# A letter for each operation in place of one drawn number per visit, in the planner that orders an attention and gated feed-forward kernel

## The chip, the cores and the metric

The kernel runs on one core of a Trainium2 chip. The metric is the device time of one execution in microseconds (us). PE is the matrix engine (TensorE), DVE is VectorE, ACT is ScalarE, POOL is GpSimd, and SP is the engine that issues nearly all DMAs. PSUM has eight banks, and every product of PE lands in one of them.

## What is computed

The reference is attention with a threshold, followed by a gated feed-forward network on its output:

```
scores = scale * np.matmul(q, k.transpose(0, 1, 3, 2))
thresh = np.max(scores, axis=-1, keepdims=True) - tau
scores = np.where(scores >= thresh, scores, -1000000000.0)
attn = np.exp(scores - np.max(scores, axis=-1, keepdims=True))
attn = attn / (np.sum(attn, axis=-1, keepdims=True) + 1e-09)
x = np.matmul(attn, v), then transposed to (B * S, H * D)
gate = 1.0 / (1.0 + np.exp(-(x @ w_gate)))
out = gate * (x @ w_val) @ w_out
```

There are 8 batches of 8 heads, 576 positions and a head size of 64; the network has 4608 tokens, a width of 512 and 1536 hidden units. All is float32.

## The kernel before

The attention is cut into 32 visits, one for a pair of heads of one batch. A visit has nine tiles of 128 query rows. For each tile PE computes scores (L641) into two PSUM banks, DVE takes the maximum (L648), ACT the exponential (L662), and DVE applies the threshold mask and sums (L665). When the tiles of a group are done, PE transposes the masked rows (L756, again into two banks), ACT copies them out (L704), and at last PE multiplies by the values (L795). A pair of banks that holds scores is free for the next tile only when L665 has read it; a pair that holds transposes is free when L704 has read it.

The network runs in between: block 0 (one batch) in whole-array matmuls at L937, block 0's output and later outputs at L866, blocks 1 and 2 at L892 in half-array matmuls where two units run side by side, the first half of one beside the second half of the other. A unit is one accumulator bank. When an L892 unit ends, ACT (L995) or ACT and DVE (L998) read its bank, and a later unit starts in that bank; the tiny copy "seen" (L904, at L866 it is L875) marks such a turn. The last six batches use a seven-product scheme (L1213, L1355) in pairs; nearly all of it stands behind the last attention work.

The order is not written by hand. Every operation is recorded with an engine, an estimated cost, its inputs and outputs, and a key (`Plan.op`). `Plan.run` then plays the operations through on estimated costs: whenever an engine is free, the ready operation with the lowest key whose buffers and banks can be had is taken, and this fixes the instruction order of each of the five engines. The chip does not see keys or costs, only the five resulting queues, each of which runs in order, and the waits between them. Two constants belong to the planner alone: `LAG`, the time it adds when a result crosses to another engine, and `SWITCH`, what it charges when PE changes between row-halved, column-halved and whole-array matmuls. `vary` sets what is added to each key between 0 and 398: in the kernel before a uniform draw between -3 and 3 from a generator seeded once per visit (`ORDERS` holds the 32 seeds, and a seed of 0 adds nothing). A step of a key is about one tile. Operations of the network on PE have keys above a million and get nothing.

Of the kernel before, what the change touches and what calls it, by code (L numbers as in the profile page):

```python
# [4 lines left out]

# [39 lines left out]
class Plan:  # L45
# [53 lines left out]
        self.ops.append(o)  # L99
        return o  # L100

    def vary(self, seed):

        draw = random.Random(seed)
        self.nudge = (lambda: draw.uniform(-NUDGE, NUDGE)) if seed else lambda: 0.0

    def room(self, o):
        need = {}
# [47 lines left out]
    def run(self):  # L156
# [10 lines left out]
        while True:  # L167
# [52 lines left out]
            while events and events[0][0] <= now + 1e-9:  # L220
# [5 lines left out]
                else:  # L226
# [6 lines left out]
                    for s in x.succ:  # L233
                        lag = 0.0 if s.eng == x.eng else LAG[s.eng]
                        s.ready = max(s.ready, now + lag + s.lag)
# [55 lines left out]
def LO_DVE(j, out):  # L291
# [2 lines left out]

DVE_LO_IN, DVE_LO_OUT = (), ()

LAG = {"PE": 0.3, "DVE": 0.06, "ACT": 0.08, "POOL": 0.12, "SP": 0.08}

WARM = 16

# [3 lines left out]
    "s": [{0, 1}, {2, 3}, {4, 5}, {6, 7}],  # L304
    "b": [{6}, {7}, {4}, {5}, {2}, {3}, {0}, {1}],
}
STAY, SWITCH, TURN = 4, 0.15, 0.0615
S_CAP, T_CAP, L_CAP, MOE_CAP = (4, 3), 1, 1, 2

MM_HALVES = 0.234  # L310
WHOLE, FULL_STEP = (0,), 6

ORDERED, NUDGE = 398, 3.0
ORDERS = (
    9752, 0, 748, 1675, 6489, 1465, 5011, 3559, 9165, 5460, 4071, 9213, 3320, 7371, 6555, 4493,
    0, 1253, 2636, 4108, 9865, 7590, 738, 2276, 1215, 1549, 3530, 2072, 647, 565, 5179, 0,
)

def LATE(b, hp):
# [1285 lines left out]
```

## Time and profile before

| | us |
|---|---|
| median of 3 runs | 1307.7 |
| lowest and highest run | 1306.86, 1309.71 |
| profiled execution, its own time | 1305.66 |
| span of its instructions | 1303.6 |
| PE busy in the span | 1265.9 |
| DVE, ACT, POOL busy | 892.8, 685.4, 512.8 |

The span is what the profile's rows are counted in; it is 2.1 us shorter than the time of the same execution, and that execution is 2.0 us below the median. PE is busy for 97% of the span.

### The profile page before, as it was taken

The page shows a single profiled execution, that of the slowest core. Times are in us where ns is not written, and L with a number is a line of the kernel's source. Part 1 is how long each engine was busy: PE and PEld are TensorE (multiplying, and loading weights), DVE is VectorE, ACT ScalarE, POOL GpSimd, SP SyncE. Part 2 cuts the span into 40 slices and gives each one's busy share as a digit, 9 for nine tenths or more (in the row PEclk, how much of TensorE's full clock was granted, in tenths as well). Part 3 has the DMA queues.
Part 4 walks back from the last instruction along what each step waited for, and adds up shares of the span by engine and source line. Part 5 has one row for each costly group of instructions (what it writes and reads, how often), then busy time and mean ns, then how long its engine had stood idle before and what let it go on. Part 6 is the DMA issues. An engine that isn't in the chain of part 4 may idle for free.

```text
span 1303.6 us, 27638 instructions
## 1 busy us (share of the span) xinstructions
PE 1265.9 (97%) x10596; PEld 997.8 (77%) x10596; DVE 892.8 (68%) x1811; ACT 685.4 (53%) x1144; POOL 512.8 (39%) x501
## 2 busy tenths in 40 slices
PE   7879999999999999999999999999999999999998
PEld 5557777777777777777777767888888888888887
DVE  7878887576776766767777774548954579555494
ACT  6877776666665656665776651224522235312242
POOL 4567777665444366584868400111001100010100
PEclk8989999999999999999999999999999999999999
DMA  7669986677655767887446668666676666765663
GB/s 284 218 216 305 337 283 218 225 263 237 234 191 180 236 222 255 288 296 227 156 146 202 222 222 295 195 201 209 221 270 195 198 206 203 232 197 188 203 208 113
DMA packets 134571, 293.17 MB, mean 225 GB/s; under 512 B 27304, under 2 KB 62376, under 8 KB 134440
## 3 DMA queue, kind: packets, MB, share of 16 engines
q1 hardware_dynamic: 134296, 291.41, 67.5%
q8 instruction: 84, 1.38, 0.4%
q14 instruction: 47, 0.39, 0.1%
q10 hardware_dynamic: 144, 0.00, 0.0%
HBM read 229.34 MB, written 62.01 MB: 224 GB/s over the span
## 4 chain that ended last, share of the span: by engine, by line
PE 86%; DMA 3%; DVE 3%; POOL 2%; ACT 2%; issue 2%; SPq 1%; DVEq 0%; POOLq 0%; ACTq 0%
PE banks L1213 26%; PE banks L1355 13%; PE banks L795 11%; PE banks L892 11%; PE banks L641 10%; PE banks L756 5%; PE banks L866 5%; PE banks L937 4%; DMA rb<-rd 1%; DVE p L665 1%; ACT pt L704 1%; DMA xa<-xf 1%; DVE st L648 1%; DMA sod<-s_o 0%; DMA qp<-in_q_dram 0%
## 5 line engine op out<-in xcount | busy, mean ns | idle before, releaser
L648 DVE TENSOR_REDUCE st<-banks 128x1 f32<-128x576 f32 x256 | 190.3, 753 | 142.3 <-PE banks L641 136.5
L665 DVE SCALAR_TENSOR_TENSOR p<-banks,st,p 128x576 f32<-128x576 f32 x256 | 205.0, 813 | 25.2 <-ACT p L662 18.3
L641 PE MATMUL banks<-kp,qp 64*128 64x288 f32 x1280 | 204.2, 424 | 12.9 <-DVE p L665 6.5
L662 ACT ACTIVATE p<-banks,st 128x576 f32<-128x576 f32 x256 | 186.7, 742 | 49.8 <-DVE st L648 48.4
L1126 POOL TENSOR_TENSOR gA<-gA 128x512 f32<-128x512 f32 x18 | 24.2, 1347 | 412.9 <-DVE gA L1192 412.9
L892 PE MATMUL banks<-x,wi 64*128 64x512 f32 x1152 | 178.6, 423 | 3.5 <-DVE g L998 2.5
L1355 PE MATMUL banks<-gs_p,wo_p 128*128 128x512 f32 x756 | 172.3, 389 | 0.0
L1355 PEld LDWEIGHTS banks<-gs_p,wo_p 128*128 128x128 f32 x756 | 141.9, 188 | 29.4
L641 PEld LDWEIGHTS banks<-kp,qp 64*128 64x128 f32 x1280 | 113.5, 189 | 49.7 <-DVE p L665 14.5
L704 ACT COPY pt<-banks 128x1024 f32<-128x1024 f32 x128 | 129.5, 1012 | 35.3 <-PE banks L756 33.3
L892 PEld LDWEIGHTS banks<-x,wi 64*128 64x128 f32 x1152 | 111.3, 186 | 25.9 <-DVE g L998 5.1
L795 PE MATMUL banks<-pt,vs 128*64 128x256 f32 x1024 | 124.7, 386 | 5.6 <-DVE p L665 3.9
L756 PEld LDWEIGHTS banks<-ident,p 64*128 64x128 f32 x2304 | 98.2, 141 | 35.3 <-DVE p L665 5.1
L1150 DVE TENSOR_TENSOR qu<-banks,qp 128x512 f32<-128x512 f32 x72 | 49.8, 692 | 92.9 <-PE banks L1213 74.4
L756 PE MATMUL banks<-ident,p 64*128 64x64 f32 x2304 | 106.1, 227 | 6.1 <-DVE p L665 2.6
L1213 PE MATMUL banks<-xs_p,wa 128*128 128x512 f32 x432 | 110.2, 390 | 0.0
L1213 PE MATMUL banks<-xs_p,wt 128*128 128x512 f32 x432 | 109.2, 389 | 0.0
L795 PEld LDWEIGHTS banks<-pt,vs 128*64 128x64 f32 x1024 | 69.9, 138 | 47.2 <-DVE p L665 5.9
L1213 PE MATMUL banks<-xs_p,ws 128*128 128x512 f32 x432 | 104.1, 390 | 0.0
L1213 PEld LDWEIGHTS banks<-xs_p,wa 128*128 128x128 f32 x432 | 80.8, 188 | 17.8 <-issue 1.2
L1213 PEld LDWEIGHTS banks<-xs_p,ws 128*128 128x128 f32 x432 | 80.9, 188 | 17.5 <-issue 0.7
L1213 PEld LDWEIGHTS banks<-xs_p,wt 128*128 128x128 f32 x432 | 81.1, 188 | 16.9
(125 smaller groups left out, 1991.0 us busy)
## 6 DMA issues: line engine op xcount, KB each, us to landing
wi<-wid SPq DMA_DIRECT2D x48, 512.0 KB
qp<-in_q_dram SPq DMA_DIRECT2D x31, 640.0 KB
wa<-wid SPq DMA_DIRECT2D x36, 512.0 KB
ws<-sid SPq DMA_DIRECT2D x36, 512.0 KB
wt<-sid SPq DMA_DIRECT2D x36, 512.0 KB
wo_p<-sod SPq DMA_DIRECT2D x36, 512.0 KB
wo_p<-wod SPq DMA_DIRECT2D x27, 512.0 KB
vs<-in_v_dram SPq DMA_DIRECT2D x32, 384.0 KB
```

The source lines that it names most:

```text
L641: nc.tensor.matmul(s.ap[:, c, :HALF], vis.q1.ap[rows, x, c0 : c0 + P], vis.k1[x].ap[rows, kc : kc + HALF], start=x == heads[0][0], stop=x ...
L648: op("DVE", 0.76, key, lambda: nc.vector.tensor_reduce(out=st.ap[:, 0:1], in_=sv(), axis=AX.XY, op=ALU.max, negate=True), reads=[s], write ...
L662: op("ACT", 0.74, key, lambda: nc.scalar.activation(p(), sv(), AF.Exp, bias=st.ap[:, 0:1], scale=1.0), reads=[s, (st, 0)], writes=[(g.p, i)])
L665: mask = op("DVE", 0.9, key, lambda: nc.vector.scalar_tensor_tensor(out=p(), in0=sv(), scalar=st.ap[:, 1:2], in1=p(), op0=ALU.is_ge, op1=A ...
L704: op("ACT", act(n), key, lambda: nc.scalar.copy(dst(), src()), reads=at, writes=[part])
L756: nc.tensor.matmul(banks[z]()[:, m * D : (m + 1) * D], p.ap[rows, o : o + P], ident[rows, rows], is_transpose=True, start=m == 0, stop=m = ...
L795: nc.tensor.matmul(av.get()[h * D : (h + 1) * D, a:z], vis.vs.ap[:, j, h], m(h), start=i == 0, stop=i == len(ms) - 1, skip_group_check=True,)
L866: nc.tensor.matmul(acc.ap, w()[h], x()[h], start=start, stop=stop, skip_group_check=True)
L892: nc.tensor.matmul(acc.ap, w()[ROWS[z]], x()[ROWS[z]], start=e == 0 and z == 0, stop=e == n - 1 and z == 1, skip_group_check=True,)
L937: nc.tensor.matmul(m.ap, wv[:, a, c * P : (c + 1) * P], xs[c].ap[:, z, c0:c1], start=e == 0, stop=e == 11,)
L1213: nc.tensor.matmul(acc.ap, wv[:, y, (2 * h + c) * P : (2 * h + c + 1) * P], xt[prod][c].get()[:, z], start=e == 0 and prod in FIRST, stop= ...
L1355: nc.tensor.matmul(acc.ap, w.ap[:, e, c, y], gt[prod][2 * g + c].get()[:, z], start=m == 0 and g == 0 and prod in FIRST, stop=m == 5 and g ...
```

## The change

Each of the 32 entries of `ORDERS` becomes a string of letters. The n-th operation of a visit with a key between 0 and 398 gets the n-th letter, where m adds nothing, a takes 3 away and z adds 3.25, in steps of a quarter; past the end of the string nothing is added. The three visits whose seed was 0 now have letters too, and the last string has 309 letters, which reach into operations behind the attention. `LAG` for PE and `SWITCH` change as well. The computation, the number of instructions on each engine and their shapes stay as they are. (The line numbers of the changed kernel are higher by 29 behind the table.)

```diff
-    def vary(self, seed):
+    def vary(self, letters):
 
-        draw = random.Random(seed)
-        self.nudge = (lambda: draw.uniform(-NUDGE, NUDGE)) if seed else lambda: 0.0
+        left = iter(letters)
+        self.nudge = lambda: (ord(next(left, "m")) - ord("m")) / 4
...
-LAG = {"PE": 0.3, "DVE": 0.06, "ACT": 0.08, "POOL": 0.12, "SP": 0.08}
+LAG = {"PE": 0.05, "DVE": 0.06, "ACT": 0.08, "POOL": 0.12, "SP": 0.08}
...
-STAY, SWITCH, TURN = 4, 0.15, 0.0615
+STAY, SWITCH, TURN = 4, 0.095, 0.0615
...
-ORDERED, NUDGE = 398, 3.0
+ORDERED = 398
 ORDERS = (
-    9752, 0, 748, 1675, 6489, 1465, 5011, 3559, 9165, 5460, 4071, 9213, 3320, 7371, 6555, 4493,
...
+    "yifoliiaqhrwhatlwpvpmmbqmbgbamnbqfynbqkoltxbdyxpivskeiptlcblmxfukujhdldgcwtlw",
...
```

The first place is the start of block 2 of the network on PE, where a unit of L892 begins in the bank of the one that has just ended: `wi2_2_1` is the new unit, `wi2_0_1` the one that ends, and the rows are the matmuls of PE's queue in the kernel before.

```order
L892 MATMUL banks_84<-x2_2_6353,wi2_0_1_5985 128x512
L892 MATMUL banks_84<-x2_3_6389,wi2_2_0_6131 128x512
L892 MATMUL banks_84<-x2_3_6389,wi2_0_1_5985 128x512
L892 MATMUL banks_84<-x2_3_6389,wi2_2_0_6131 128x512
L892 MATMUL banks_84<-x2_3_6389,wi2_0_1_5985 128x512
L892 MATMUL banks_84<-x2_3_6389,wi2_2_0_6131 128x512
L892 MATMUL banks_84<-x2_3_6389,wi2_0_1_5985 128x512
L892 MATMUL banks_84<-x2_0_3571,wi2_2_1_6200 128x512
```

No other matmul stands between the last one of `wi2_0_1` and the first of `wi2_2_1`. The same place of PE's queue in the changed kernel:

```order
L921 MATMUL banks_84<-x2_3_6246,wi2_0_1_5934 128x512
L670 MATMUL banks_84<-kp4_2_1_5572,qp4_2_5579 128x288 x2
L670 MATMUL banks_84<-kp4_3_0_5781,qp4_3_5950 128x288 x2
L670 MATMUL banks_84<-kp4_3_1_5941,qp4_3_5950 128x288 x2
L785 MATMUL banks_84<-ident_71,p4_2_00_6324 128x64 x2
L785 MATMUL banks_84<-ident_71,p4_2_10_6438 128x64 x2
L921 MATMUL banks_84<-x2_0_3627,wi2_2_1_6079 128x512
```

Here the scores of three tiles and four small transposes of visits in batch 4 stand between the two.

The second place is PE's first visit, right behind its warm-up matmuls. The queue counts two matmuls for a tile's scores, where the trace has four. In the kernel before (`kp_0_0` and `kp_0_1` are the keys of the visit's two heads, `p_0_00` the masked rows of its first group, `p_0_l` those of its leftover tile):

```order
L641 MATMUL banks<-kp_0_0_229,qp_0_231 128x288 x10
L641 MATMUL banks<-kp_0_1_235,qp_0_231 128x288 x4
L756 MATMUL banks<-ident,p_0_00_267 128x64 x16
L641 MATMUL banks<-kp_0_1_235,qp_0_231 128x288 x6
L756 MATMUL banks<-ident,p_0_l_337 128x64 x10
L756 MATMUL banks<-ident,p_0_02_281 128x64 x16
```

And in the changed kernel:

```order
L670 MATMUL banks<-kp_0_0_229,qp_0_231 128x288 x10
L670 MATMUL banks<-kp_0_1_235,qp_0_231 128x288 x2
L785 MATMUL banks<-ident,p_0_00_267 128x64 x16
L670 MATMUL banks<-kp_0_1_235,qp_0_231 128x288 x6
L785 MATMUL banks<-ident,p_0_02_281 128x64 x16
L670 MATMUL banks<-kp_0_1_235,qp_0_231 128x288 x2
L785 MATMUL banks<-ident,p_0_l_328 128x64 x10
```

The first transposes stand one tile earlier, those of the second group come ahead of the leftover tile's, and one tile of scores stands between these two.

## Rows read from the trace of the kernel before

**Rows 1.** The page: the span, and busy time, share and instructions of each engine.

```profile
span 1303.6 us, 27638 instructions
...
PE 1265.9 (97%) x10596; PEld 997.8 (77%) x10596; DVE 892.8 (68%) x1811; ACT 685.4 (53%) x1144; POOL 512.8 (39%) x501
```

**Rows 2.** Busy time by stretch; after POOL: granted clock of PE, DMA share, GB/s.

```profile
0.00:12.00 12.00, 8.08 (x60) 6.42 (x60) 6.19 (x18) 6.25 (x10) 1.96 (x10) 1.00 0.82 276
12.00:24.00 12.00, 9.18 (x90) 6.28 (x90) 9.25 (x20) 7.75 (x13) 7.37 (x15) 0.72 1.02 408
24.00:78.00 54.00, 40.72 (x530) 28.61 (x526) 46.36 (x102) 44.08 (x70) 33.29 (x53) 0.99 0.60 199
78.00:92.00 14.00, 12.72 (x136) 9.00 (x136) 9.66 (x21) 8.79 (x16) 9.17 (x11) 0.69 0.59 199
92.00:205.00 113.00, 112.51 (x852) 79.62 (x853) 93.21 (x189) 84.86 (x137) 84.59 (x80) 1.00 0.90 305
205.00:763.00 558.00, 548.45 (x6449) 429.38 (x6448) 389.31 (x949) 363.70 (x617) 326.06 (x300) 1.00 0.67 222
763.00:810.00 47.00, 44.64 (x328) 33.54 (x328) 24.68 (x49) 13.89 (x22) 1.82 (x2) 1.00 0.77 278
810.00:1304.00 494.00, 489.57 (x2160) 404.93 (x2158) 314.11 (x472) 156.10 (x264) 48.52 (x36) 1.00 0.63 203
```

**Rows 3.** Waits of PE, 0 to 92 us: total us, times, longest.

```profile
PE banks L641 <- DVE p L665: 5.6, 4, 1.9
PE banks L795 <- DVE p L665: 3.9, 2, 2.6
PE banks L641 <- ACT pt L704: 3.1, 3, 1.1
PE banks L430 <- POOL ident masks.py:199: 1.4, 1, 1.4
```

**Rows 4.** Timeline of PE, 83.8 to 90 us: start, us, what.

```profile
83.88 3.37 PE L795 MATMUL banks<-pt,vs 128*64 128x256 f32 x16
...
87.52 1.89 PE L795 MATMUL banks<-pt,vs 128*64 128x256 f32 x16
```

**Rows 5.** Waits of PE, 205 to 763 us.

```profile
PE banks L892 <- DVE g L998: 2.5, 6, 0.8
PE banks L866 <- ACT seen L875: 2.3, 5, 1.3
PE banks L892 <- ACT th L995: 1.0, 3, 0.5
```

**Rows 6.** Timeline of PE around the first place: start, us, what, idle before it.

```profile
477.73 0.86 PE L892 MATMUL banks<-x,wi 64*128 64x512 f32 x6
479.40 1.66 PE L892 MATMUL banks<-x,wi 64*128 64x512 f32 x12 [0.81 <-DVE g L998]
```

**Rows 7.** Groups by line: busy us, mean ns of one, idle before.

```profile
L665 DVE SCALAR_TENSOR_TENSOR p<-banks,st,p 128x576 f32<-128x576 f32 x256 | 205.0, 813 | 25.2 <-ACT p L662 18.3 <-DVE st L657 0.5
L648 DVE TENSOR_REDUCE st<-banks 128x1 f32<-128x576 f32 x256 | 190.3, 753 | 142.3 <-PE banks L641 136.5 <-PE banks L756 2.4 <-ACT p L662 2.0
L662 ACT ACTIVATE p<-banks,st 128x576 f32<-128x576 f32 x256 | 186.7, 742 | 49.8 <-DVE st L648 48.4
L704 ACT COPY pt<-banks 128x1024 f32<-128x1024 f32 x128 | 129.5, 1012 | 35.3 <-PE banks L756 33.3 <-DVE st L657 0.6 <-DVE p L665 0.4
```

**Rows 8.** The chain that ended last, in order of time: start, us, what.

```profile
39.71 1.26 PE banks L641 x8
...
92.31 1.66 PE banks L937 x6
...
762.83 1.58 PE banks L1213 x6
...
774.29 0.04 issue
...
899.56 2.72 PE banks L1213 x12
```

More of the change, by code (lines that the diff above doesn't have):

```diff
@@ L2 @@
 import itertools
-import random
 from contextlib import ExitStack
@@ L311 @@
 WHOLE, FULL_STEP = (0,), 6
-ORDERED, NUDGE = 398, 3.0
+ORDERED = 398
 ORDERS = (
-    9752, 0, 748, 1675, 6489, 1465, 5011, 3559, 9165, 5460, 4071, 9213, 3320, 7371, 6555, 4493,
-    0, 1253, 2636, 4108, 9865, 7590, 738, 2276, 1215, 1549, 3530, 2072, 647, 565, 5179, 0,
+    "yifoliiaqhrwhatlwpvpmmbqmbgbamnbqfynbqkoltxbdyxpivskeiptlcblmxfukujhdldgcwtlw",
+    "qpaqegqkudcpdrkyrkwyrvciebmbpgxeltvuqwmoruqejhmtolmpkvejwtrgtplrsjusbgwpypvoorm",
+    "qrqsxbcgcuxugkcgwhqjdqwglpnxwuiudibmltwcboktqmskpasinstqiievsrbxqsfbtexlmgyktxqasim",
+    "krunpvwngqhvppsuaiqkhyrewjudgmqsxwslrkyrvwitdjjbquiwbmckokkksmybmujjiudtfljnrdgytyxibkipbcmbdwgnqpp",
+    "npgtauiqnkrnsfkeuqhjjaaviwkspdkweyosgbbqehgjwcefylvqwiinedbkibwyarhdvgyyiaexbbtcmhh",
+    "mxohprchytoehwfdhcmkvumxfkmssewxhiyufbcdwkhvynjjaxfqhhfifyrongxtgkapgygeqvmmchbsfco",
+    "uaijwayuvibdrkjfnkjopddxcyabrydbswsqiquacnvkeundjxeuhklrqexhfybppyblpclxvkvqvkqqeeb",
+    "njfpgykmvorcqvehxonharybehpvssxhnhtxwysjacfiyckqqeqbhvyfjknvsfvsuxihcohblkeqxlqwrxhbqdnfjcxiidhnhjiratadto",
+    "ojrsdrtutleegkssobdthkricccnfghrbsgnyuffdnthmppxvrmpthvtjxifrvaulvneaedcpdvfikbfl",
+    "gidbmuipjyrhyiwoscqqynexypvcofhtvosbcnjuwoiutdnvkxbvspbdqiokcdefaitfakeebsiarnkfi",
+    "wrsccudyaclrmedarborriopjqvdysnwpcrlvxivociwlwnfdhbgmjrxrmrhwknxuxddlmqbtmkebthfg",
+    "exdjxsxuiftlfhpfouhgelxwaumbecjihfmmqnaohhidwarkomjrgueqaxtsjflehjuavmitiohhoquistcynryktrgwperhvudikndsjefecsysljdrj",
+    "pctcllihnsbakjaejxembbflpnnrjuhmtnbgqugrabtrojxjlfqugiodrvjxikngurqahdqlpkgegpmvx",
+    "ijrcubmynfuxhajrytukxtuprjpfcmrlgastmboenjtfnbxirmybysskkoisbgbvtxougbvtuormfgwxi",
+    "ewfhekckruxdlrahdsinlmoledholqfmtrdnrrffxpcdkhiuxvbpxsjgscctkljlwhlnlghtjwnexfafs",
+    "ltmblmqsbrulcdwbuovifflakoovaqbdmncrgmlnircooootogipsotfkxhiiqwkdigiynqgkaihrahyf",
+    "xrgjifytxhsmqqcckfyfungkheceahtixipwmsvxbneqcveemtwrmfiljgwyswecfjvcbwfngcfkpdoyu",
+    "vwgsbijahhdfgtpgrldyknqvttfoiolfoodlqbeqfhaoehyqjdwcmigpkjjylvoqogjxuprdsighxygsm",
+    "ckrrdeiiepnslcrorejmyynsenbskhddhpklletbjauspdatylpvvypmjnoohuqajkfgtagffthnkalle",
+    "cdjrmwvhyefsnaqtiqhxmokwjdkwahwmpenoibwsdlfkwurlagbwdoxdckosranlgorowhxjptapthxfoknwmdubuqxiwwgqafbmjumjakcmeviexgdditnlpkkhorytpeygeudhiih",
+    "coigbhcdhhisvqihvumaxdoonaeplaxkbjipwmlhhiymwjmcmflnajlssbtnelbtdootscxnkulmlisye",
+    "swpcuraqnkhiadytygpqboxrodlvayjblasqirpmwkrxfkemoliipukdjqxkdeshygvewiwtglulhsgun",
+    "qmkgkbbddprrqlubpkdssokgvicsretcxxddmkvdkhdmpwlsjowmnsyclpqntlfrgrucbqrldkfgvcppu",
+    "pqcbslrfeekgdlwlwmfbsornlrqxgmwmyjfrywloabosuokxhcxyyraeubopxreyquddmtcxkxfufbvtm",
+    "obhbuejlohspdybphlvdwhthoqlrqnpmgsfucuvkgghybymdrevpqxvvcrkkahhnyedheacfgsxorsjcc",
+    "uuveibrwhlvlfctfygdmhaqblyjhtlakfvmqjgbxitckqnkxbpdowrmbjnqlevulftesrgxklngkcfuwg",
+    "lwhecmlhxqsipxmamqshvuwfrqlqianlqjetwseofctvbghcalrydwfmmmlcmujghmiqbtcupxiuomxvp",
+    "dxrvxpqkfqyqliayssikaihyannvkknludivdnaddimxaysvfcybohvbbedasuwsyrwtvmlmqrofqiexf",
+    "wjxwbturqjrbynircpecescxthuiymfowcglasxaaxmjjonwfxcwfsnxfkywalajdkxpdmnngvpyjhgrc",
+    "mdnrnyegkwlcmcuwpaotppguinlyaiaektktnihphsbumrvjcydsgvkdxmchkysxiuslwafoefibyvgom",
+    "enpluxwottxscesfwfwrmlvjjwvrgscfwjmpvnwearqrlpijnenklimivnavorcnlbnfwypbvjcfrjhmi",
+    "cmflcudqnvpradedudungqfsiiqrjhgdivikjqhluwjxiefkbhqrbdcmaqtjeuacrvouqeulcroknyywdujagcaupqlbnmndvvsefoambkveehthiwceqeqneryyeqiubbugmbedxyiylmagfhisquwnpejhvtkruiedyatpilcosvlndcttrfctvicihbyayhiyusmkygfmripgglrsdnddqokqnpwbgikmurifduixbsfprgdcjfclcypnoklmwpaoacaffudsuwjtyulaoxmtnfwwrbdpuaggjjnnqsrqynxtowejc",
```

## Prediction

> **What bounds the kernel now.** The page comes first: PE is busy for 1265.9 us of a span of 1303.6, DVE for 68% and the others for less [rows 1]. The reader should see that PE is the bound and that 37.7 us of it are idle. The same instructions run on PE after the change, in the same number and shapes, so apart from its clock only this idle time can move. The busy times by stretch say where it lies [rows 2]. Before 92 us PE is busy for 8.08 + 9.18 + 40.72 + 12.72 = 70.7 us, so 21.3 are idle; 92 to 205 us leaves 0.5; 205 to 763 us leaves 9.6; 763 to 810 us leaves 2.4; the rest leaves 4.4, nearly all of it behind the last matmul. From 810 us on there is no attention work left and the letters have nothing to mix, so I leave those 494 us as they are. What can move is the opening and the stretch from 205 to 763 us.
>
> The waits of PE in the opening show a loop [rows 3]: scores wait for the mask of an earlier tile (5.6 us) or for the copy of earlier transposes (3.1 us), because only four pairs of banks exist; value products wait for masks too (3.9 us). The 1.4 us at the first line are the program's start. DVE is busy there for 6.19 + 9.25 + 46.36 + 9.66 = 71.5 of 92 us, ACT for 66.9, so neither is full: PE waits for them and they wait for PE. Its clock is low in two stretches, 0.72 from 12 to 24 us and 0.69 from 78 to 92 us [rows 2], a mix of 2.4 and 1.2 GHz, and each comes behind idle time of PE (3.9 us of the first 12, for one). What that costs is seen in two equal groups of products: 3.37 us at 83.88 and 1.89 us at 87.52 [rows 4].
>
> From 205 to 763 us the waits have other names [rows 5]: L892 waits nine times for the bank of a unit that has just ended (2.5 us on DVE, 1.0 on ACT), L866 five times for the turn copy (2.3 us). The largest is 0.81 us at 479.40 [rows 6].
>
> **The change, part by part.** The two constants are the planner's picture of PE and cost nothing on the chip. The row at 774.29 puts 0.04 us between the end of a mask on DVE and PE's start on its transposes [rows 8]; the planner assumed 0.3 and now assumes 0.05. Six L1213 matmuls between attention pieces take 1.58 us, and 1.36 (half of 2.72) in a run of their own [rows 8], which makes 0.11 for each of the two switches around them; the planner goes from 0.15 to 0.095. Both move towards the trace. Counted in the two PE queues there are 143 switches before and 142 after, so switching itself gives 0.1 us, which I count as nothing.
>
> *L892 units.* I counted in PE's queue the work between the end of a unit and the first matmul of the unit that takes its bank, at 0.63 us for a tile of scores (1.26 for eight matmuls is two tiles [rows 8]). In the kernel before, eleven units start with at most one tile in between, and the nine waits fall on nine of these: the one with nothing in between is the 0.81 us [rows 6]. Units with a tile and sixteen transposes between (some 1.1 us) have no wait. In the changed queue all units have at least that; at the first place shown three tiles and four transposes, some 2.0 us, cover the 0.81. So I take all of it: 2.5 + 1.0 = 3.5 us. What was in between elsewhere may be missed there; but then some unit would be left short, and none is. Bounds: 3.0 to 3.5.
>
> *L866 turns.* Before, three of thirteen starts have at most a few transposes in front of them; after, none has fewer than sixteen, some 0.5 us. But one start of before that had as many still waited 1.3 us, the longest of the row [rows 5], so cover of that size is not safe. I take 1.2 of the 2.3 us; bounds 0.6 and 2.3.
>
> *Opening.* PE sets off what it later waits for. From scores to the mask's end it is 0.75 + 0.74 + 0.81 us in the three engines [rows 7], with their hand-overs some 2.5; from transposes to the copy's end 1.01 [rows 7], some 1.15. I counted where PE's queue holds less work than that between cause and use. Up to the first matmul of the network: 35 such places before, lacking 24.6 us in all, and 34 after, lacking 18.7. The measured idle without the program's start is some 19.6 us, 0.8 of the count, so the difference of 5.9 would be 4.7. The second place shown is one: with four pairs of banks, the earlier transposes let ACT's copy start a tile sooner. This count leaves out the queues of DVE and ACT, which have the same work to do in those 92 us and can hand the wait on: a mask that PE no longer waits for is only followed by one it does. I take 3.0, between 0 (they set the pace, at 78% and 73% busy) and 5.9. The place before 83.88, behind which the clock falls, looks alike in both queues, so I leave the clock's loss where it is.
>
> *92 to 205 us.* The same count finds 1.7 us before, where 0.5 was measured, and 3.5 after: places where scores follow transposes too closely. I add 0.8 us; bounds 0.5 and 1.8. *763 to 810 us:* the transposes of the last visits lacked 0.6 us before and 1.1 after; I add 0.3, bounds 0 and 0.6.
>
> *Other queues.* The number of instructions on DVE, ACT, POOL and SP is unchanged too. Weight loads are chained in their own order, and no PE wait in [rows 3] or [rows 5] is for a DMA, so moved DMAs cost nothing as long as the loads run ahead as they do now; DMA is busy for 0.67 of 205 to 763 us [rows 2], which leaves room.
>
> Sum: -3.5 - 1.2 - 3.0 + 0.8 + 0.3 = -6.6 us. The profiled execution took 1305.66, so 1299.1 for one like it. It lay 2.0 below the median of the three runs; against 1307.7 the same step gives 1301.1, which I predict.
>
> **Rivals.** *The low-clock stretch goes (faster still).* The 14 us at 0.69 and the 12 at 0.72 lose 0.31 x 14 = 4.3 and 0.28 x 12 = 3.4 us of clock, less what PE waits in them anyway. If the waits ahead of 83.88 get shorter and PE stays at 2.4 GHz, some 3.9 us more are gained: 1297.2. For it speaks the smaller count of shortfalls; against it that the queue ahead of that place is nearly the same. The Trainium skill ("TensorE: Matmul & The Clock Gate", What's actually happening) says that the clock is gated by how busy PE has recently been; the falls behind idle PE in this trace agree.
>
> *A third low-clock stretch (slower).* The same mechanism with the other sign. If the new opening leaves PE with one more wait like its longest (2.6 us [rows 3]) at a point where the others don't shrink, and the clock falls behind it as it did at 78 us (4.3 us), the opening costs 6.9 us where I count a gain of 3.0. With -4.7 from the later waits and +1.1 that makes +3.3: 1311.0. It decides once the opening loses more than 3.6 us. For it: the count says nothing of DVE's and ACT's queues, and the clock falls twice already. Against it: 34 places lacking less, spread evenly.
>
> *Waits only change their names (no change).* PE's idle time from 205 to 763 us is 1.7% of that stretch. If the covered unit starts only pass the wait to scores and transposes behind them, and DVE and ACT set the pace of the opening, the gain is 0 to 2.5 us: some 1306.5. For it: the same tiles must get through the same four pairs of banks. Against it: filling a gap with ready work leaves no gap elsewhere while ready attention work is to be had, and the units without a wait show that it usually is.
>
> **How the numbers follow.** Three runs of the kernel before lie 2.9 us apart, 0.2%; less than that can't be told from no change. It puts "faster" below 1305.1 and "slower" above 1310.3. Chances: the forecast (1298 to 1305) 0.60, the clock gained 0.13, no change 0.17, the third stretch 0.10. Faster is 0.60 + 0.13 = 0.73, same 0.17, slower 0.10. All bounds at their good end give -3.5 - 2.3 - 5.9 + 0.5 + 0 = -11.2, and -15.1 with the clock; at their bad end -3.0 - 0.6 - 0 + 1.8 + 0.6 = -1.2. The range for 8 in 10 leaves out the upper rival and the far end of the lower: 1295.5 to 1307.5.
>
> **What would show it.** In the changed profile PE's waits of L892 for L995 and L998 should be gone (under 0.5 us for 3.5), those of L866 for L875 about halved, and PE idle before the first network matmul some 18 us for 21.3, that matmul starting near 89 us rather than at 92.3 [rows 8]; PE's busy time from 205 us on should be the same. If the first network matmul starts as late as now, the opening was paced by DVE and ACT. If the L892 waits go and the end doesn't come sooner, another wait took their place, and the list of PE's waits will name it. A granted clock under 0.8 in a stretch other than the two would show the slower rival. I would be wrong by more than the range if a queue other than PE's came to set the pace in the middle, most likely a late weight load.

## The result and the profile after

The changed kernel takes 1289.59 us (median of four runs, 1288.04 to 1291.55), the kernel before, run beside it, 1307.28 (1304.38 to 1309.71). The ratio is 0.9866, interval 0.984 to 0.9893: 17.7 us less, where 6.6 were forecast and 1295.5 was the lower end of the range. The profiled execution took 1288.04 us, its span is 1286.3, so its span is 17.3 shorter than the one of [rows 1]. Line numbers of the changed kernel are those of before plus 29 (L892 is now L921, L866 is L895, L641 is L670, L756 is L785, L795 is L824, L937 is L966).

The page of the changed kernel, span and engines:

```profile
span 1286.3 us, 27688 instructions
...
PE 1259.8 (98%) x10596; PEld 1001.6 (78%) x10596; DVE 892.5 (69%) x1811; ACT 684.2 (53%) x1144; POOL 512.3 (40%) x501
```

Against [rows 1] PE is idle for 26.5 us in place of 37.7, which is 11.2 us of the gain. The other 6.1 us came out of PE's *busy* time, from 1265.9 to 1259.8, with the same 10596 matmuls. That is the surprise of this case. In the middle alone (the last three stages of the table below) it is 8.8 us of idle and 6.7 of busy time.

Busy time by stretch in the changed kernel, in the stretches of [rows 2] (columns as there):

```profile
0.00:12.00 12.00, 7.93 (x62) 6.25 (x62) 6.21 (x18) 6.45 (x10) 1.81 (x10) 1.00 0.80 277
12.00:24.00 12.00, 8.31 (x72) 5.71 (x74) 8.21 (x17) 7.52 (x12) 6.50 (x14) 0.75 1.02 409
24.00:78.00 54.00, 44.14 (x544) 30.64 (x543) 46.83 (x101) 44.16 (x68) 32.97 (x53) 0.94 0.56 177
78.00:92.00 14.00, 12.84 (x156) 8.88 (x156) 11.33 (x28) 11.14 (x19) 9.68 (x11) 0.95 0.70 241
...
205.00:763.00 558.00, 556.41 (x6596) 442.20 (x6596) 401.55 (x976) 370.58 (x627) 328.75 (x304) 1.00 0.69 229
```

From 205 to 763 us PE has 1.6 us idle, where it had 9.6. The low clock has moved: 0.69 from 78 to 92 us has become 0.95, and 24 to 78 us went from 0.99 to 0.94.

The same microsecond holds other work in the two kernels, so I cut both executions where a stage of PE begins: the first matmul of L937, of L866, of L892, of the pair's output (L866 again), and of L1213. First the stretches of before by this cut (columns as in [rows 2]), then those of after:

```profile
0.00:92.30 92.30, 70.70 (x812) 50.31 (x812) 71.76 (x157) 67.15 (x106) 52.09 (x86) 0.91 0.68 236
92.30:212.40 120.10, 119.91 (x924) 84.91 (x925) 97.41 (x200) 90.39 (x146) 90.21 (x85) 1.00 0.85 288
212.40:290.90 78.50, 76.33 (x882) 58.55 (x878) 51.41 (x129) 48.45 (x81) 53.10 (x53) 1.00 0.73 244
290.90:631.00 340.10, 334.06 (x3930) 263.90 (x3926) 234.15 (x568) 216.12 (x379) 183.70 (x175) 1.00 0.70 234
631.00:762.70 131.70, 130.36 (x1576) 101.40 (x1572) 98.95 (x243) 93.16 (x149) 83.04 (x69) 1.00 0.59 188
```

```profile
0.00:90.30 90.30, 71.52 (x817) 50.33 (x817) 71.28 (x159) 67.59 (x105) 50.21 (x85) 0.92 0.67 229
90.30:210.80 120.50, 119.57 (x910) 85.27 (x910) 98.61 (x200) 88.85 (x146) 88.32 (x82) 1.00 0.89 302
210.80:286.90 76.10, 75.93 (x918) 62.18 (x914) 53.20 (x132) 50.70 (x86) 55.40 (x56) 1.00 0.73 244
286.90:616.90 330.00, 329.46 (x3892) 262.80 (x3894) 231.51 (x562) 214.42 (x377) 184.63 (x176) 1.00 0.72 241
616.90:745.60 128.70, 128.70 (x1582) 101.83 (x1578) 99.02 (x244) 92.51 (x149) 82.38 (x68) 1.00 0.59 191
```

Stage by stage the change gives -2.0 (opening), +0.4 (block 0 in), -2.4 (block 0 out), -10.1 (blocks 1 and 2 in) and -3.0 us (the pair's output); what follows is 540.8 and 540.6 long. The three last stages of the table hold 6388 matmuls before and 6392 after, and take 550.3 and 534.8 us. These 15.5 us are where the forecast had 4.7.

Not all of PE's waits of this stretch stand in [rows 5]. The view of before has five more, 3.3 us in all, and four of them are of scores:

```profile
PE banks L641 <- issue: 1.0, 1, 1.0
PE banks L641 <- DVE p L665: 0.9, 2, 0.6
PE banks L641 <- ACT pl L704: 0.5, 1, 0.5
PE banks L641 <- ACT seen L904: 0.5, 1, 0.5
```

In the three stages of after one wait of PE is left:

```profile
PE banks L921 <- ACT ot L1065: 0.2, 1, 0.2
```

Why PE's busy time fell is seen at L892. The view of one line's instructions adds PE's idle time and that of the weight loads (PEld) ahead of it, by what ended it; L892 before, PE and PEld together:

```profile
L892 PE MATMUL banks<-x,wi x1152: 383/392/610, 290.9 to 622.8; 64*128 64x512 f32 x192
...
  DVE g L998: 7.5, 17
  ACT th L995: 4.0, 11
```

and L921 after:

```profile
L921 PE MATMUL banks<-x,wi x1152: 382/392/610, 286.9 to 608.9; 64*128 64x512 f32 x192
...
  ACT th L1024: 1.8, 7
  ACT ot L1065: 0.9, 2
  DVE g L1027: 0.5, 2
```

Before, 17 + 11 = 28 entries of 11.5 us are counted here. PE's matmuls have 9 of them with 3.5 us [rows 5], so the weight loads have 19 with 8.0. One wait can stand in both: at 479.40, the place of [rows 6], the load waits 1.25 us and its matmul 0.81.

```profile
479.40 1.23 PEld L892 LDWEIGHTS banks<-x,wi 64*128 64x128 f32 x12 [1.25 <-DVE g L998]
```

After, the entries come to 3.2 us, and 0.2 of these are PE's. A matmul is drawn as busy to its modelled end, 392 ns in the median, but six of them in three pairs take 0.86 us [rows 6], so that the next pair starts (0.86 - 0.39) / 2 = 0.23 us after the last. A wait shorter than the rest, some 0.16 us, is drawn as busy time of PE, and from a longer one that much is missing.

The time from the start of one matmul to the start of the next leaves nothing out. I summed it from the traces over the three stages, by the line of the matmul at the end of each interval; "in front of" a line means this sum here and below. Of the 15.5 us, 5.7 went in front of L892, 4.6 in front of L866 and 6.1 in front of scores (8 of their 948 matmuls lie in other stages after; at 1.26 / 8 us each [rows 8] they are some 1.3 of the 6.1). In front of transposes, of which 20 more lie here, 1.3 us were added, and 0.3 went in front of value products. So scores, which the forecast had at nothing, gave about as much as either kind of unit.

### The profile page after: what moved, and what is told of

Its sections match the earlier page's. It is cut to its first block, busy times and chain, and to the rows that moved or that the text cites. A ratio compares the mean times of both kernels' runs of the same rounds, so it can differ in the third digit from the quotient of the medians.

```text
span 1286.3 us, 27688 instructions
## 1 busy us (share of the span) xinstructions
PE 1259.8 (98%) x10596; PEld 1001.6 (78%) x10596; DVE 892.5 (69%) x1811; ACT 684.2 (53%) x1144; POOL 512.3 (40%) x501
## 4 chain that ended last, share of the span: by engine, by line
PE 95%; DVE 2%; ACT 1%; issue 1%; DMA 1%; POOL 0%; DVEq 0%; POOLq 0%
PE banks L1242 27%; PE banks L1384 13%; PE banks L670 12%; PE banks L824 12%; PE banks L921 11%; PE banks L895 7%; PE banks L785 7%; PE banks L966 6%; ACT pt L733 1%; DVE st L677 1%; DMA qp<-in_q_dram 1%; DVE p L694 1%; DMA tau_t<-in_tau_dram 0%; ACT p L691 0%; POOL qp L650 0%
## 5 line engine op out<-in xcount | busy, mean ns | idle before, releaser
L670 PE MATMUL banks<-kp,qp 64*128 64x288 f32 x1280 | 204.4, 424 | 9.8 <-DVE p L694 3.9
L921 PE MATMUL banks<-x,wi 64*128 64x512 f32 x1152 | 176.1, 420 | 0.3 <-ACT ot L1065 0.2
L670 PEld LDWEIGHTS banks<-kp,qp 64*128 64x128 f32 x1280 | 118.0, 190 | 43.0 <-ACT pt L733 7.2
L785 PEld LDWEIGHTS banks<-ident,p 64*128 64x128 f32 x2304 | 98.2, 141 | 38.3 <-DVE p L694 5.7
L921 PEld LDWEIGHTS banks<-x,wi 64*128 64x128 f32 x1152 | 112.2, 186 | 20.1 <-ACT th L1024 1.8
L824 PE MATMUL banks<-pt,vs 128*64 128x256 f32 x1024 | 123.4, 383 | 0.2 <-DVE p L694 0.2
L785 PE MATMUL banks<-ident,p 64*128 64x64 f32 x2304 | 106.5, 227 | 8.6 <-POOL st L686 2.7
L1242 PE MATMUL banks<-xs_p,wt 128*128 128x512 f32 x432 | 109.4, 390 | 0.0
L824 PEld LDWEIGHTS banks<-pt,vs 128*64 128x64 f32 x1024 | 69.2, 137 | 41.4 <-issue 4.2
L1242 PEld LDWEIGHTS banks<-xs_p,wa 128*128 128x128 f32 x432 | 80.8, 188 | 17.8 <-DMA rd<-turned 0.4
```

The costliest lines, as they stand in the source:

```text
L670: nc.tensor.matmul(s.ap[:, c, :HALF], vis.q1.ap[rows, x, c0 : c0 + P], vis.k1[x].ap[rows, kc : kc + HALF], start=x == heads[0][0], stop=x ...
L785: nc.tensor.matmul(banks[z]()[:, m * D : (m + 1) * D], p.ap[rows, o : o + P], ident[rows, rows], is_transpose=True, start=m == 0, stop=m = ...
L824: nc.tensor.matmul(av.get()[h * D : (h + 1) * D, a:z], vis.vs.ap[:, j, h], m(h), start=i == 0, stop=i == len(ms) - 1, skip_group_check=True,)
L921: nc.tensor.matmul(acc.ap, w()[ROWS[z]], x()[ROWS[z]], start=e == 0 and z == 0, stop=e == n - 1 and z == 1, skip_group_check=True,)
L1242: nc.tensor.matmul(acc.ap, wv[:, y, (2 * h + c) * P : (2 * h + c + 1) * P], xt[prod][c].get()[:, z], start=e == 0 and prod in FIRST, stop= ...
```

## The experiments

**Theory A** is the prediction's: the letters do it, by giving PE work between a unit's end and the unit that takes its bank, and by a denser opening. **Theory B**: the planner's two constants do it. Later, **theory C**: all bank waits of the middle, those of attention and of the units, are one flow and hand on to one another; **rival D**: the 10 us lie in how PE's own rows alternate, whatever they wait for. Ratios are to the kernel before on the same chip. The stages of all runs, cut as above (the start of the first matmul of each stage, subtracted; us):

| kernel | opening | block 0 in | block 0 out | blocks 1, 2 in | pair's output | rest |
|---|---|---|---|---|---|---|
| before | 92.3 | 120.1 | 78.5 | 340.0 | 131.8 | 540.8 |
| after | 90.3 | 120.5 | 76.1 | 330.0 | 128.7 | 540.6 |
| e1 constants alone | 104.5 | 116.3 | 77.4 | 356.7 | 143.1 | 534.1 |
| e2 letters alone | 107.9 | 119.4 | 84.5 | 353.0 | 131.0 | 535.2 |
| e4 shuffled letters | 109.4 | 118.2 | 79.1 | 358.8 | 126.4 | 552.5 |
| e6 seeds in the opening | 103.0 | 116.1 | 80.1 | 331.2 | 128.7 | 540.5 |
| e7 before, early release | 93.0 | 120.0 | 80.8 | 338.9 | 131.6 | 540.6 |
| e8 after, early release | 90.9 | 120.5 | 76.1 | 330.6 | 128.7 | 540.5 |
| e9 after, late release | 92.9 | 120.5 | 76.1 | 344.3 | 128.7 | 540.9 |
| e10 before, mask cut | 97.0 | 122.9 | 83.3 | 349.3 | 138.7 | 542.4 |
| e11 before, all cut | 95.3 | 122.3 | 81.3 | 346.9 | 138.8 | 541.3 |
| e12 after, all cut | 96.7 | 120.8 | 79.9 | 347.2 | 135.9 | 540.7 |
| e13 before, short vector | 82.3 | 119.9 | 78.5 | 330.2 | 130.4 | 540.5 |
| e14 after, short vector | 82.0 | 120.5 | 76.0 | 326.5 | 128.4 | 539.9 |

### Which half of the edit: e1, e2, e4, e6

e1 is the kernel before with the two constants of the change and the old seeds:

```
-LAG = {"PE": 0.3, "DVE": 0.06, "ACT": 0.08, "POOL": 0.12, "SP": 0.08}
+LAG = {"PE": 0.05, "DVE": 0.06, "ACT": 0.08, "POOL": 0.12, "SP": 0.08}
...
-STAY, SWITCH, TURN = 4, 0.15, 0.0615
+STAY, SWITCH, TURN = 4, 0.095, 0.0615
```

> The kernel before with its 32 seeds, but with the changed LAG (0.05) and SWITCH (0.095). Theory A (the letters themselves, by what stands in front of a unit's start): its queue has 22 starts of L892 with less than 1 us of PE work since the end of the unit whose bank they take, where the kernel before has 11 and the changed one none; the stretch from the first L892 matmul to the first output matmul of the pair took 340.1 us before and 330.0 after, 0.9 us for each of the 11, so this kernel is slower than before by some 10 us or more, 1315 to 1330. Theory B (the planner's constants): most of the 18 us, 1288 to 1297.

Measured: 1334.57 us, ratio 1.0207 (1.0186 to 1.0228). Theory B falls: the constants alone cost 27 us. The time lies above theory A's range too (1315 to 1330): the opening alone is 12.2 us longer, which the count of unit starts doesn't see. The same holds for e2 and e4 below (15.6 and 17.1 us in the opening).

e2 is the other half, the letters with the old constants (the two lines above the other way round, on the changed kernel):

> The changed kernel with its letters but with LAG 0.3 and SWITCH 0.15 as before. Theory A: 18 short starts of L892, so some 6 us or more above the kernel before, 1310 to 1325, though the letters are the same, because they fit one queue only. Theory B: as the kernel before, 1303 to 1311. A third theory (letters are good in any queue): as the changed kernel, 1288 to 1297.

Measured: 1334.9 us, ratio 1.0217 (1.0195 to 1.0239). Neither half gives anything; the letters fit one setting of the planner. A letter always belongs to the same operation, but which other operations are ready beside it, and so what its shift of the key does, depends on the planner's constants.

e4 is the changed kernel with the letters of each string in a random order:

```
-    "yifoliiaqhrwhatlwpvpmmbqmbgbamnbqfynbqkoltxbdyxpivskeiptlcblmxfukujhdldgcwtlw",
+    "pptmcxlifrtaocqtbkhibyknilbmowldiyqfgvlnukbsbjwpwxebqymmpavtxlwhifqblgdmdulah",
...
```

> The changed kernel with the letters of each string put in another order at random, constants as changed. Theory A: 23 short starts, 1315 to 1330. Theory B, or that any finer mixing does it: 1288 to 1297.

Measured: 1346.14 us, ratio 1.03 (1.0285 to 1.0315). It is these letters at these places, not finer mixing in itself: 57 us lie between them and the same letters shuffled. In blocks 1 and 2 its waits of PE are

```profile
PE banks L921 <- DVE g L1027: 7.2, 10, 1.2
PE banks L921 <- ACT th L1024: 2.7, 7, 0.9
```

where the changed kernel has 0.2 in all.

e6 is the changed kernel with the four seeds of before in place of the first four strings (the visits of the opening):

```
-    "yifoliiaqhrwhatlwpvpmmbqmbgbamnbqfynbqkoltxbdyxpivskeiptlcblmxfukujhdldgcwtlw",
...
+    9752,
+    0,
+    748,
+    1675,
```

> The changed kernel with the first four visits on the seeds of before (and the changed constants), the letters in the other 28. No short start of L892; the opening's shortfalls count 27.0 us against 19.2 in the changed kernel. Theory A: the middle as in the changed kernel, the opening longer by 2 to 6 us: 1291 to 1297. Rival (a better opening is what carries the rest): at least half of the gain is lost, 1298 to 1308.

Measured: 1302.56 us, ratio 0.997 (0.9957 to 0.9983). The time lies where the rival put it, and most of the 17.7 us is lost. But from blocks 1 and 2 on it is as after (331.2 and 128.7), so these stages keep their gain without the letters of the opening. The opening is 103.0, 12.7 longer than after, where 2 to 6 were expected; block 0 in is 4.4 shorter and block 0 out 4.0 longer. This opening is not that of before: with the new constants the old seeds give another order, nearly that of e1 (PE's first 568 matmuls stand in the same order in the queues of both, and e1's opening is 104.5). So e6 does not price what the change did to the opening, which is the 2.0 us by stage. Two of its stretches:

```profile
24.00:92.00 68.00, 50.70 (x548) 34.23 (x544) 52.89 (x110) 49.47 (x79) 42.43 (x61) 0.84 0.70 227
92.00:103.00 11.00, 9.57 (x120) 7.07 (x116) 7.86 (x16) 7.16 (x14) 6.99 (x7) 0.89 0.56 185
```

PE idles for 17.3 of the 68 us and its granted clock is 0.84 in them, so it has part of them at 1.2 GHz. Over the opening the clock is 0.88 (0.91 before); the price of this order is thus waits with the clock on top.

### The unit starts: e7, e8, e9

In all three the queues of the engines are unchanged. In e7 (from before) and e8 (from after) the tanh and the gate's product read only 64 of 512 columns from the bank, and make the other 448 from another operand in SBUF:

```
+nc.scalar.activation(th.ap[:, :EDGE], m.ap[:, :EDGE], AF.Tanh, scale=0.5)
+nc.scalar.activation(th.ap[:, EDGE:], f32(xs[0].ap[:, 0, EDGE:]), AF.Tanh, scale=0.5)
...
+for c, src in ((slice(0, EDGE), m.ap), (slice(EDGE, SM), th.ap)):
+    nc.vector.scalar_tensor_tensor(
+        out=g[f].ap[:, z, c], in0=th.ap[:, c], scalar=1.0, in1=src[:, c], op0=ALU.add, op1=ALU.mult)
```

> The kernel before, all five queues in the same order, but the evictions of L892 (L995, L998) are cut in two: 64 columns that read the bank, and 448 columns that read SBUF instead, so that the bank comes free some 0.5 us sooner and the engines work as long as before. (It leaves out the gate and value of 448 columns of each unit of blocks 1 and 2.) Theory A (PE's losses in the middle are waits at the starts of units): the stretch from the first L892 matmul to the first output matmul of the pair falls from 340 to 330 to 334 us, the time to 1297 to 1301. Rival (the losses are those of the attention work between, its masks and copies): it falls by less than 2 us, 1304 to 1308.

> The same cut (64 columns from the bank, 448 from SBUF, so the same columns left out) in the changed kernel. Theory A: there are no waits at starts left to shorten, the stretch stays at 329 to 331 us, the time at 1287 to 1291. Rival (a sooner release helps whatever the order): 4 us or more off.

Measured: e7 1305.71 us, ratio 0.9982 (0.9967 to 0.9997); e8 1289.38, ratio 0.987 (0.985 to 0.989). e7's waits of PE in blocks 1 and 2 (291 to 631 us):

```profile
PE banks L643 <- issue: 2.0, 1, 2.0
PE banks L643 <- DVE p L667: 0.9, 2, 0.7
PE banks L643 <- ACT pl L706: 0.5, 1, 0.5
PE banks L643 <- ACT seen L906: 0.5, 1, 0.5
PE banks L894 <- DVE g L1005: 0.3, 1, 0.3
```

Of the 3.5 us of unit starts 0.3 are left (L894 is L892), and yet the stage is only 1.1 us shorter. Scores (L643 is L641) wait more instead: from start to start the time in front of L892 matmuls falls by 4.5 us in this stage (138.6 to 134.1), and 3.3 of these come back in front of scores (69.9 to 72.2) and transposes (52.9 to 54.0). So in the old order the unit starts alone are worth 1.1 us in this stage of the profiled execution, and 2.4 (interval 0.4 to 4.3) by the times: theory A's price for them falls, and the rival "waits only change their names" was right about this one edit. In e8, where no such wait was left, the time stays (1289.38 for 1289.59), as theory A said.

e9 goes the other way: the changed kernel, with an eviction of the same length from SBUF ahead of each of these two, so that every unit's bank comes free later; what is computed stays.

```
+nc.scalar.activation(th.ap, f32(xs[0].ap[:, 0]), AF.Tanh, scale=0.5)
 nc.scalar.activation(th.ap, m.ap, AF.Tanh, scale=0.5)
...
+for src in (th, m):
```

> The changed kernel, queues in the same order, with an eviction of the same length that reads SBUF put ahead of each L995 and L998, so that the bank comes free some 0.6 us later (and DVE has 17 us, ACT 14 us more to do in 330 us; the result is the same). Theory A: the shortest covers, some 1.1 us of PE work, are then too short; 22 of 46 starts wait some 0.3 us and more: the stretch grows by 4 to 12 us, 1294 to 1302. Rival (starts don't matter much): less than 2 us, 1287 to 1292.

Measured: 1303.34 us, ratio 0.9968 (0.9954 to 0.9982). The stage goes from 330.0 to 344.3 and its waits of PE are

```profile
PE banks L921 <- ACT th L1026: 4.7, 12, 0.5
PE banks L921 <- DVE g L1032: 3.1, 4, 1.2
```

The 14.3 us are nearly twice the 4.7 + 3.1 that PE shows, and more than the 4 to 12 that theory A expected. From start to start 13.3 of them stand in front of L921 matmuls (132.4 to 145.8). The cover of unit starts matters, then: losing it costs at the starts themselves, while gaining it in e7 was handed on. The added evictions also keep DVE and ACT busy for longer (253.4 us for 231.5, 227.7 for 214.4 in this stage); how much of the 14.3 is due to that, the run does not tell.

### The whole flow: e10 to e14

e10 cuts the read of the mask (L665) in the kernel before: 64 of 576 columns come from the banks, the other 512 are made from what SBUF holds. e11 (before) and e12 (after) add the cuts of e7 and the same for the copies of transposed tiles (L704): the first 64 columns of each bank from there, the rest from SBUF.

```
+nc.vector.scalar_tensor_tensor(
+    out=p()[:, :, :32], in0=sv()[:, :, :32], scalar=st.ap[:, 1:2], in1=p()[:, :, :32], ...)
+nc.vector.scalar_tensor_tensor(
+    out=p()[:, :, 32:], in0=p()[:, :, 32:], scalar=zero_t[:, 0:1], in1=p()[:, :, 32:], ...)
...
+nc.scalar.copy(dst[:, :, :1], tp.ap[:, :, : w // 2].rearrange("p z (k q) -> p z k q", q=D)[:, :, :1])
+nc.scalar.copy(pt.ap[:, P:w], p.ap[:, : w - P])
```

> The kernel before with the same queues, but the mask of a score tile (DVE, L665) reads only 64 of its 576 columns from the score banks and the other 512 from SBUF, so that the banks come free about 0.6 us sooner; the gate's and value's work is untouched (the mask's result is wrong for 512 columns of 576). Theory C (what is left of blocks 1 and 2, the 340.0 us of which the change took 10 and the early gates only 1, is made of waits of the attention work for the bank pairs, which hand on to one another): the segment of blocks 1 and 2 falls to 334-338 and the time to 1296-1304. Rival D (the 10 us are in PE's own rows: how the instructions alternate, not what they wait for): segment 339-341, time 1305-1310.

> The kernel before with the same queues and all the long reads of the banks cut short: mask (64 columns of 576), the copies of transposed tiles (the first 64 columns of each bank), and the evictions of gate and value in blocks 1 and 2 (64 of 512); the rest of each is read from SBUF, so it is wrong there. Theory C: with all of them gone together the segment of blocks 1 and 2 falls from 340.0 to 329-334, as after the change, and the time to 1285-1298. Rival D: segment 337-340, time 1303-1308, since the waits were never the larger part.

> The changed kernel with the same three cuts. Its segment of blocks 1 and 2 is 330.0 with hardly a wait left in it, so both theories expect little: C 327-330 and a time of 1280-1290; D 329-331. What it measures is the floor of the segment, against which the cut kernel before is read.

Measured: 1334.37 (ratio 1.0204, 1.0178 to 1.0229), 1326.61 (1.0153, 1.013 to 1.0177) and 1320.97 (1.0106, 1.0085 to 1.0128), all slower than the kernels that they come from. As a test of C they failed, since the cut lengthened what it was to shorten. DVE in e10, the two parts of the mask:

```profile
L672 DVE SCALAR_TENSOR_TENSOR p<-p,zero_t 128x512 f32<-128x512 f32 x256 | 255.9, 1000 | 0.0
...
L668 DVE SCALAR_TENSOR_TENSOR p<-banks,st,p 128x64 f32<-128x64 f32 x256 | 71.4, 279 | 22.2 <-ACT p L664 15.4 <-DVE st L659 0.5
```

The mask takes 1.28 us for 0.81 [rows 7], and DVE is busy for 1000.6 us in place of 892.8. That is a finding too: 108 us more on an engine that is busy for 68% of the span, with 70 more on POOL, cost some 27 us.

e13 (before) and e14 (after) mend this: the mask is done on 64 columns and left out for the other 512, and the second part of the gate's product is a plain copy of one operand; the copies and the tanh are cut as in e11.

```
+mask = op("DVE", 0.9, key, lambda: nc.vector.scalar_tensor_tensor(
+    out=p()[:, :, :32], in0=sv()[:, :, :32], scalar=st.ap[:, 0:1], in1=p()[:, :, :32], ...)
...
+nc.vector.tensor_copy(g[f].ap[:, z, EDGE:], th.ap[:, EDGE:])
```

> The kernel before with the same queues; the mask is done on 64 of the 576 columns of a score tile and left out for the other 512 (0.28 us on DVE in place of 0.81), the copies of transposed tiles and the evictions of gate and value in blocks 1 and 2 read 64 columns a bank from the banks and the rest from SBUF, in forms that don't take DVE longer than before. So the banks come free sooner and DVE has about 140 us less to do, which the cuts of the masks before this one had the wrong way round. Theory C (waits of attention and unit starts that hand on to one another): the segment of blocks 1 and 2, 340.0 before, falls to 328-333, and the time to 1280-1295. Rival D (the 10 us are in PE's own rows, whatever they wait for): segment 336-340, time 1298-1306.

> The changed kernel with the same cuts: the floor of the segment of blocks 1 and 2, 330.0 after. C and D both: 326-330; time 1270-1288. If C holds, the two shortened kernels differ by under 4 us in that segment, where the kernels themselves differ by 10.1; if D holds, by 7 or more.

Measured: 1284.29 us (ratio 0.9818, 0.9788 to 0.9849) and 1275.88 (0.9744, 0.9722 to 0.9765). The opening and the stage of blocks 1 and 2 in e13, then that stage in e14 (columns as in [rows 2]):

```profile
0.00:82.30 82.30, 65.13 (x812) 47.16 (x812) 52.14 (x157) 67.81 (x126) 52.08 (x86) 1.00 0.77 265
...
280.70:610.80 330.10, 328.90 (x3922) 265.53 (x3924) 165.59 (x591) 223.91 (x475) 182.62 (x174) 1.00 0.71 239
```

```profile
278.40:605.00 326.60, 326.52 (x3896) 260.93 (x3896) 169.45 (x583) 221.84 (x472) 185.56 (x176) 1.00 0.73 244
```

With PE's queue of before, the stage falls from 340.0 to 330.2, and the two shortened kernels differ in it by 3.7 us where the kernels themselves differ by 10.1. C expected 328 to 333 and a difference under 4, D 336 to 340 and 7 or more: C holds against D. From start to start the time in front of L892 matmuls is 134.1 us, as in e7, but now that of scores falls as well, from 69.9 to 65.0, instead of taking the units' gain over. Two things changed at once, though: the banks come free sooner, and DVE is busy for 741.6 us in place of 892.8. Which of the two did it is not separated. PE's idle time in this stage fell from 6.0 to 1.2 us, and its busy time from 334.1 to 328.9 on practically the same matmuls (3930 and 3922 records), so the half that is drawn as busy was waiting time too.

Over the three stages from 212 to 763 us, 550.3 becomes 539.1 in e13 and 534.8 becomes 530.9 in e14: of the 15.5 us between the kernels 8.2 are left. From start to start 5.4 of the 8.2 stand in front of L866 matmuls, where the cuts changed next to nothing (83.8 us before, 84.3 in e13, 78.9 in e14), and 2.9 in front of L892; scores and transposes cancel. Part of the 5.4 is the turn copy, which no cut touched. Block 0 out in e13, waits of PE:

```profile
PE banks L872 <- ACT seen L881: 1.7, 2, 1.4
PE banks L898 <- ACT ot L1050: 0.3, 1, 0.3
```

(L872 is L866.) By stage the 8.2 are 2.5 (block 0 out), 3.7 and 2.0, and by the windows of these stages about half of it, 4.0, is idle time of PE that e13 still has and e14 has not. Some work has moved between the stages as well: blocks 1 and 2 hold 26 transposes fewer after, some 0.8 us at the prediction's 0.5 for sixteen, and block 0 out 40 more. No run takes the turn copy away, so how the rest of the 8.2 us divides between it and what rival D means stays open.

## Why the prediction was wrong, by its steps

The direction was right and the place too: PE's waits in the opening and the middle. What failed is one sentence of the first part, "apart from its clock only this idle time can move", and with it the price of the middle, 4.7 us where 15.5 were measured: 8.8 came out of idle time and 6.7 out of what is drawn as busy, which the prediction held fixed ("PE's busy time from 205 us on should be the same"). The second failure is a term put at nothing without a reason: the waits of scores in this stretch, 2.9 us on PE, which [rows 5] leave out. In front of scores 6.1 us went, some 4.8 of them not because scores moved.

- **L892 units, -3.5.** The waits went as said: 0.2 us are left of 3.5 on PE, and none of that on L995 or L998. But the stage lost 10.1 us. The term was mis-sized: over the three stages 5.7 us went in front of L892. It was taken at the length that PE's idle column shows, where the weight loads of this line had 19 waits of 8.0 us and PE nine of 3.5. Most of what the stage lost beside that went in front of scores. That the nine waits had a price of their own, removable one by one, is refuted by e7 (1.1 us in the stage). The count of units that start uncovered was a good sign, not a price. The same count on the other orders goes with the stage: 0 uncovered (less than 1 us of PE's work in between) at 330.0 and 331.2 (after, e6), 11 at 340.0 (before), 18, 22 and 23 at 353.0, 356.7 and 358.8 (e2, e1, e4). As the starts in front of scores moved too, the count is at best a sign of how tightly the whole flow through the banks is packed; e13 agrees with that, but no run shows the count itself to be the cause.
- **L866 turns, -1.2.** PE's waits for L875 are gone, not halved. The two stages that hold these units, block 0 out and the pair's output, lost 2.4 and 3.0 us, and the first of them with 36 more matmuls in it. From start to start 4.6 us went in front of L866, so the term of 1.2 and its upper bound of 2.3 were too low, again by being read from PE's idle column.
- **Opening, -3.0.** The first matmul of L937 starts at 90.3 us, not near 89, and PE is idle before it for 90.3 - 71.5 = 18.8 us, some 18 being forecast: -2.0 in all. Near enough (the idle time that the term was scaled by is 21.3 - 1.4 = 19.9 us, not 19.6, which changes nothing). The count of shortfalls in PE's queue ranked the three openings rightly (18.7 us after, 24.6 before, 27.0 in e6) but not their distances: e6 has 2.4 more than before and is 10.7 us longer, with a lower clock (0.88 for 0.91), which the count leaves out.
- **The clock's loss of the opening, unchanged.** The low stretch from 78 to 92 us went (0.95), another came (0.94 from 24 to 78 us), and over the opening the clock is 0.91 before and 0.92 after. The sum was right and the place was not. e13 shows the stake: with DVE quicker the granted clock is 1.00 throughout, and its opening is 10.0 us shorter, idle time (21.6 to 17.2 us) and clock together. The Trainium skill ("TensorE: Matmul & The Clock Gate", What's actually happening) has the clock follow how busy PE has been; the falls behind idle PE agree. How long PE idles in sum does not tell: e13 idles for 17.2 of 82.3 us at 1.00, e14 for 14.9 of 82.0 at 0.98.
- **Block 0 in, +0.8, and 763 to 810 us, +0.3.** The first measured +0.4, the stretch behind the pair's output -0.2: both small, as forecast.
- **The constants cost nothing on the chip.** Right, no instruction reads them. But they decide what the letters mean: either half without the other costs 27 and 28 us (e1, e2).
- **The rivals.** "Waits only change their names" is what the single edit e7 does, and not what the change does, because the change re-orders the whole flow. The range's lower bound was made of the same idle column; even all bounds at their good end with the clock gained, -15.1, fall short of the 17.7.

## What to carry to other kernels

Where PE is the bound and its instructions overlap, price waits from the queue of weight loads as well as from PE's idle column, without adding the two up, and take the difference of stage lengths (first matmul to first matmul), or the time from start to start by line, as the measure. A wait for a bank in a tight flow has no price of its own: ask what the flow would do with all of them gone (here 9.8 us of a stage, with DVE's work shortened too), and with this one gone (1.1 us). Here an order found for one setting of the planner was worth nothing under another, and planner constants nearer to the trace were no improvement by themselves.

## What was not expected of the hardware

In e10 GpSimd slowed down together with DVE. Its scaling of queries, first in before and then in e10:

```profile
L621 POOL TENSOR_SCALAR qp<-qp,scale_t,zero_t 128x640 f32<-128x640 f32 x58 | 50.6, 881 | 54.4 <-DMA qp<-in_q_dram 44.4 <-PE banks L756 8.5 <-PE banks L641 1.5
```

```profile
L623 POOL TENSOR_SCALAR qp<-qp,scale_t,zero_t 128x640 f32<-128x640 f32 x58 | 58.6, 1018 | 40.4 <-DMA qp<-in_q_dram 36.3 <-PE banks L765 3.9 <-PE banks L901 0.2
```

The same instruction takes 1018 ns for 881, and GpSimd's busy time goes from 512.8 to 582.3 us, once the mask reads two operands from SBUF (in e13, where it does not, 879 ns and 513.0 us); DVE itself takes 1000 ns for 512 such columns where 576 with one operand in the banks took 813 [rows 7]. The Trainium skill ("GPSIMD Engine Reference", Specifications) says that GpSimd shares its SBUF interfaces with VectorE and that they contend when VectorE has two SBUF inputs; the trace agrees. Reading from SBUF rather than from a bank is therefore no cheap way to free the bank here.
